# PSUM split, load order, single-tile groups, planned transfer times, PE transposes and zero matmuls in a fused attention and two-matrix kernel

## The chip, the cores and the metric

The kernel runs on one core of one Trainium2 chip. The metric is the device time in microseconds (us). Most quoted times are medians of several runs. Ratios to the kernel before are computed as the mean time of one kernel's fast runs over the mean time of the other's fast runs of the same rounds, so they are not quite the ratio of the medians. The profile shows the span from the first to the last instruction, which is about 1.8 us shorter than the device time.

PE is TensorE, ACT is ScalarE, DVE is VectorE, POOL is GpSimd, SP is SyncE. A "tile" in the text is a block of 128 tokens; there are 24 of them (4 batches of 768 tokens), numbered 0 to 23.

## The reference, cut to what matters

```python
# q, k, v: (4, 8, 768, 64)   w_in: (512, 2048)   w_out: (2048, 512)
scores = q @ k.T / 8 + bias                 # keep only the last 96 keys and the first 8
a = softmax(scores)
x = (a @ v) as (3072 tokens, 512)
h = x @ w_in                                # the "first matrix"
out = (h - tanh(h)) @ w_out                 # the "second matrix"
```

Because only the last 96 keys count, a tile's queries meet the keys of their own tile and of the tile before. So each tile has one or two blocks of scores for 8 heads.

## The kernel before

The kernel describes all its work as operations with an engine, a modelled duration, what they wait for and which buffers they take and give. A planner in the kernel (plain Python, run when it is built) simulates this and so fixes the order of instructions on each engine. Engines work strictly in that order. If the plan thinks that a transfer is done sooner than it is, PE stands before an instruction that can't run yet, though other work behind it could.

```python
groups = [[0, 1], [2, 3], [4, 5]] + [[u, u + 1, u + 2] for u in range(6, NU, 3)]
ps_big = ... bufs=3    # [P, 2, 512] fp32: two banks each
ps_sm  = ... bufs=1    # one bank: transposes, late AV
ps_op  = ... bufs=1    # one bank: second-matrix output, early AV
PE_T = 6               # tiles 0-5: q/k and x are transposed by PE, the rest by DMA
# ... cut ...
def m1(g, f0):         # first matrix of one group: a chunk fills two banks
    n, per, m = shape1(g)
    t = hs[g, f0] = ps_big.tile([P, 2, 512], FP32, name="big")
    # ... per f: CD = 4 matmuls over the contraction
# ... cut ...
AHEAD = 5.5
T_DT, T_DX = 1.0, 0.5                 # the plan's time of a q/k and of an x transpose by DMA
T_LD, T_W, T_ST = 1.15, 3.15, 0.7
before = [("t", 0), ("t", 1), ("t", 2), ("in", 0), ("t", 3), ("in", 1), ("in", 2), ("in", 3),
          ("out", 0), ("out", 1), ("t", 4), ("out", 2), ("out", 3), ("t", 5)]
```

The list `before` is the order of loads: `t` is a tile's q, k and v (3 x 256 KB), `in` and `out` are quarters of the two weight matrices. The first matrix of a group can start when x of all its tiles has been transposed. The Trainium skill, "PSUM — Partial Sum Buffer", section "Specifications (TRN2)", gives 8 banks of 2 KiB per partition. The kernel uses all of them: 3 x 2 + 1 + 1.

The softmax here doesn't subtract the row's maximum and nothing guards it: scores larger than these inputs give would overflow.

Of the kernel before, what the change touches and what calls it, by code (L numbers as in the profile page):

```python
# [16 lines left out]
def kernel(  # L17
# [14 lines left out]
    P = 128  # L32
# [15 lines left out]
    PE_T = 6  # L48
    TMAX = 3


    groups = [[0, 1], [2, 3], [4, 5]] + [[u, u + 1, u + 2] for u in range(6, NU, 3)]
# [13 lines left out]
    ps_big = ctx.enter_context(tc.tile_pool(name="ps_big", bufs=3, space=bass.MemoryType.PSUM))  # L66
    ps_sm = ctx.enter_context(tc.tile_pool(name="ps_sm", bufs=1, space=bass.MemoryType.PSUM))
    ps_op = ctx.enter_context(tc.tile_pool(name="ps_op", bufs=1, space=bass.MemoryType.PSUM))
# [4 lines left out]
    tmp01 = cpool.tile([P, P], FP32, name="tmp01")  # L73
# [9 lines left out]
    def build_masks():  # L83
        r0, r1, r2 = rmat[:, 0, :], rmat[:, 1, :], rmat[:, 2, :]
        nc.gpsimd.iota(
            r1, pattern=[[1, P]], base=0, channel_multiplier=-1,
            allow_small_or_imprecise_dtypes=True,
        )
        nc.gpsimd.tensor_copy(out=tmp01, in_=r1)
        nc.gpsimd.iota(  # L90
            r2, pattern=[[1, P]], base=P, channel_multiplier=-1,
            allow_small_or_imprecise_dtypes=True,
        )
        for dst, fill in ((r1, BIG), (tmp01, float(L))):
            nc.gpsimd.affine_select(
                dst, dst, pattern=[[1, P]], base=0, channel_multiplier=-1,
                compare_op=ALU.is_ge, fill=fill,
            )
            nc.gpsimd.affine_select(
                dst, dst, pattern=[[-1, P]], base=L - 1, channel_multiplier=1,  # L100
                compare_op=ALU.is_ge, fill=fill,
            )
        nc.gpsimd.affine_select(
            r2, r2, pattern=[[-1, P]], base=L - 1 - P, channel_multiplier=1,
            compare_op=ALU.is_ge, fill=BIG,
        )
        nc.gpsimd.memset(rmat[0:G, 2, :], float(L))
        nc.gpsimd.tensor_copy(out=r0, in_=r1)
        nc.gpsimd.tensor_copy(out=rmat[0:G, 0, :], in_=tmp01[0:G, :])
        for h in range(H):  # L110
            slope = 2.0 ** (-8.0 * (h + 1) / H)
            nc.scalar.activation(mk[:, slot(h), :, :], rmat, AF.Exp, bias=0.0, scale=-slope)
# [57 lines left out]
    def a_T(u):  # L170
        tr[u] = ps_sm.tile([P, 2, NP, P], BF16, name="sm")
        for j in (1, 0):
            for p in range(NP):
                nc.tensor.transpose(tr[u][:, j, p, :], kq[u][:, j, p * P : (p + 1) * P], ident)  # L174
# [7 lines left out]
    def a_Te(u):  # L182
        qk[u] = kpool.tile([P, 2, NP, P], BF16, name="qk")
        nc.vector.tensor_copy(out=qk[u], in_=tr.pop(u))
# [24 lines left out]
    def a_AV(u, part):  # L209
        h0 = part * (H // 2)  # L210
        pool, nm = (ps_op, "op") if u < AV_OP else (ps_sm, "sm")
        t = pool.tile([P, H // 2, Dh + 1], FP32, name=nm)
        for h in range(H // 2):
            last = u % NQ == 0
            nc.tensor.matmul(  # L215
                t[:, h, :], pr[u, 0][:, slot(h0 + h), :], vb[u % NV][:, h0 + h, :],
                start=True, stop=last,
            )
            if not last:
                nc.tensor.matmul(  # L220
                    t[:, h, :], pr[u, 1][:, slot(h0 + h), :], vb[(u - 1) % NV][:, h0 + h, :],
                    start=False, stop=True,
                )
        av[u, part] = t

    def a_R(u, part):
        h0 = part * (H // 2)
        if part == 0:
            xs[u] = xpool.tile([P, H, Dh], BF16, name="x")
        t = av.pop((u, part))  # L230
        rden = xpool.tile([P, H // 2, 1], FP32, name="rden")
        nc.vector.reciprocal(rden, t[:, :, Dh : Dh + 1])  # L232
        nc.vector.tensor_tensor(  # L233
            out=xs[u][:, h0 : h0 + H // 2, :], in0=t[:, :, 0:Dh],
            in1=rden.to_broadcast([P, H // 2, Dh]), op=ALU.mult,
        )

    def a_V(u):
        nc.gpsimd.tensor_copy(
            out=vb[u % NV][0:G, :, 0:Dh], in_=vb[(u - u % NQ) % NV][0:G, :, 0:Dh]  # L240
        )

    def a_X(u):
        x = xs[u].rearrange("q h d -> q (h d)")
        tr[u, "x"] = ps_sm.tile([P, CD, P], BF16, name="sm")
# [3 lines left out]
    def x_dst(u):  # L249
        g = group_of[u]  # L250
        if g not in xT:
            xT[g] = tpool.tile([P, CD, TMAX * P], BF16, name="xT")
        o = (u - groups[g][0]) * P
        return xT[g][:, :, o : o + P]
# [8 lines left out]
    gs, hs, ths, os_, ots = {}, {}, {}, {}, {}  # L263

    def shape1(g):
        n = len(groups[g]) * P
        per = 512 // n
        return n, per, min(2 * per, FJ)

    def m1(g, f0):  # L270
        n, per, m = shape1(g)
        t = hs[g, f0] = ps_big.tile([P, 2, 512], FP32, name="big")
        for f in range(f0, f0 + m):
            j, fo = f // FJ, (f % FJ) * P
            a, o = (f - f0) // per, ((f - f0) % per) * n
            for c in range(CD):
                nc.tensor.matmul(  # L277
                    t[:, a, o : o + n], w_in_bf[j][:, c, fo : fo + P], xT[g][:, c, 0:n],
                    start=(c == 0), stop=(c == CD - 1),
                )  # L280

    def h_view(t, g):
        n, per, m = shape1(g)
        per = min(per, m)
        return t[:, 0 : m // per, 0 : per * n].rearrange("q a (b n) -> q a b n", n=n)

    def m1_th(g, f0):
        ths[g, f0] = hpool.tile([P, 2, 512], FP32, name="th")
        nc.scalar.activation(h_view(ths[g, f0], g), h_view(hs[g, f0], g), AF.Tanh, bias=0.0, scale=1.0)  # L289

    def m1_g(g, f0):
        n, per, m = shape1(g)
        if g not in gs:
            gs[g] = gpool.tile([P, CF, TMAX * P], BF16, name="g")
        dst = gs[g][:, f0 : f0 + m, 0:n].rearrange("q (a b) n -> q a b n", b=min(per, m))
        nc.vector.tensor_tensor(  # L296
            out=dst, in0=h_view(hs.pop((g, f0)), g), in1=h_view(ths.pop((g, f0)), g), op=ALU.subtract,
        )

    def m2(g, t, qq):  # L300
        u = groups[g][t]
        if qq == 0:
            pool, nm = (ps_sm, "sm") if tail_sm(u) else (ps_op, "op")
            os_[u] = pool.tile([P, DM], FP32, name=nm)
        for f in range(qq * 4, qq * 4 + 4):
            nc.tensor.matmul(  # L306
                os_[u], gs[g][:, f, t * P : (t + 1) * P], w_out_bf[f // FJ][:, f % FJ, :],
                start=(f == 0), stop=(f == CF - 1),
            )

    def tail_sm(u):
        return u == NU - 2
# [5 lines left out]
    def store(u):  # L318
# [3 lines left out]
    AV_OP = 4  # L322
    AHEAD = 5.5
    T_DT, T_DX = 1.0, 0.5
    T_LD, T_W, T_ST = 1.15, 3.15, 0.7
    before = [("t", 0), ("t", 1), ("t", 2), ("in", 0), ("t", 3), ("in", 1), ("in", 2), ("in", 3),
              ("out", 0), ("out", 1), ("t", 4), ("out", 2), ("out", 3), ("t", 5)]
# [4 lines left out]
    for u in range(6, NU):  # L332
        gate_of["ld", "kf", u] = ("ld", "kf", u - 1)
    for n, it in enumerate(before):
        if n >= 2 and (it[0] == "t") != (before[n - 1][0] == "t"):
            gate_of[("ld", "kf", it[1]) if it[0] == "t" else it] = landed(before[n - 2])
    for it in before:
        if it[0] != "t":
            kind, j = it
            op(it, POOL, 0.8, (lambda j=j: load_w_in(j)) if kind == "in" else (lambda j=j: load_w_out(j)),  # L340
               after=[gate_of.get(it)], dma=T_W, pri=-1)
    w_order = [it for it in before if it[0] != "t"]
    for a, b in zip(w_order, w_order[1:]):
        ops[b]["after"].append(("issue", a))
# [3 lines left out]
    for g, us in enumerate(groups):  # L348
        n, per, m = shape1(g)
# [4 lines left out]
    tiles = [it[1] for it in before if it[0] == "t"]  # L354
    tiles += [u for u in range(NU) if u not in tiles]
    prev = None
    for u in tiles:
        i = u % NQ
# [5 lines left out]
    for u in range(NU):  # L364
        i = u % NQ
        e0 = DVE if u == 0 else POOL
        op(("ck", u), e0, 0.62, lambda u=u, e=e0: cast(u, 1, kf, nc.vector if e is DVE else nc.gpsimd),
           after=[("ld", "kf", u)], take=["kq"], give=["kf"])
        op(("cq", u), e0, 0.62, lambda u=u, e=e0: cast(u, 0, qf, nc.vector if e is DVE else nc.gpsimd),
           after=[("ld", "qf", u), ("ck", u)], give=["qf"])  # L370
        op(("cv", u), POOL, 0.62, lambda u=u: cast_v(u),
           after=[("ld", "vf", u), ("AV", u - NV + 1, 1) if u >= NV else None,
# [3 lines left out]
        if u < PE_T:  # L376
            op(("T", u), PE, 0.46, lambda u=u: a_T(u), after=tdep, take=["sm"], give=["kq"])
            op(("Te", u), DVE, 0.69, lambda u=u: a_Te(u), after=[("T", u)], give=["sm"])
        else:
            op(("T", u), SP, 0.3, lambda u=u: a_DT(u), after=tdep, give=["kq"], dma=T_DT)  # L380
        te = ("Te", u) if u < PE_T else ("T", u)
# [6 lines left out]
        if 1 <= i < NQ - 1:  # L388
            op(("K", u), DVE, 0.2, lambda u=u: a_K(u), after=[("S", u, 0)])
            op(("V", u), POOL, 0.61, lambda u=u: a_V(u), after=[("AV", u, 1)])  # L390
        for part in range(2):
            bank = "op" if u < AV_OP else "sm"
            op(("AV", u, part), PE, 0.25, lambda u=u, part=part: a_AV(u, part),
               after=[("M", u, 0), ("M", u, 1) if i else None, ("cv", u),
                      ("V", u - 1) if i >= 2 else None, ("AV", u, 0) if part else None],
               take=[bank], give=(["p0", "p1"] if i else ["p0"]) if part else [])
            op(("R", u, part), DVE, 0.63, lambda u=u, part=part: a_R(u, part), after=[("AV", u, part)],
# [150 lines left out]
```

## Time and profile before

| | before |
|---|---|
| device time, median of 3 (range) | 239.92 us (238.84 to 241.54) |
| span of the profiled run | 238.6 us |
| PE busy | 205.2 us (86%) |
| last matmul ends | 234.7 us |

Below are lines from the page's first two parts: the busy time of each engine, then PE, granted TensorE clock and DMA in tenths over 40 slices of the span, about 6 us each.

```profile
PE 205.2 (86%) x1712; PEld 122.6 (51%) x1736; DVE 127.4 (53%) x238; ACT 111.5 (47%) x137; POOL 64.9 (27%) x111
...
PE   1476876999999669979896997999999999999993
...
PEclk9999799999999999999999999999999999999999
DMA  7998998999999999899999999543342111111112
```

The windows view sums up stages. Its columns are the window, its length, then busy time (and number of instructions) of PE, weight loads, DVE, ACT, POOL, the granted clock, the DMA share and GB/s.

```profile
0.00:20.00 20.00, 9.16 (x98) 6.40 (x99) 9.75 (x30) 9.61 (x14) 11.52 (x28) 1.00 1.05 184
20.00:50.00 30.00, 24.65 (x237) 18.79 (x238) 16.49 (x28) 11.52 (x12) 9.55 (x15) 0.94 1.10 189
50.00:80.00 30.00, 27.18 (x276) 17.56 (x280) 18.86 (x38) 15.15 (x18) 13.73 (x22) 1.00 1.24 225
80.00:120.00 40.00, 33.94 (x323) 19.66 (x325) 26.41 (x52) 21.44 (x26) 14.89 (x24) 1.00 1.03 209
120.00:160.00 40.00, 36.16 (x308) 20.54 (x311) 23.80 (x46) 21.59 (x27) 13.39 (x21) 1.00 1.05 194
160.00:200.00 40.00, 39.63 (x305) 22.36 (x308) 22.48 (x39) 20.01 (x25) 1.83 (x3) 1.00 0.26 67
```

PE is the bound from 160 us on. Before that it waits: 10.8 us of the first 20, and 9.9 us between 80 and 160 us (80 less 33.94 and 36.16). DMA is busy until 150 us.

Busy does not mean fast. These are lines of the timeline (start, length, engine, line, operation, tiles, shape, count, and in brackets the idle time before and what ended it):

```profile
11.54 1.04 PE L192 MATMUL big<-qk 64*128 64x128 bf16 x16 [0.57 <-DVE qk L184]
...
19.72 3.24 PE L277 MATMUL big<-xT,w_in_bf_98 128*128 128x256 bf16 x16 [0.63 <-DVE xT L257]
...
43.02 1.91 PE L277 MATMUL big<-xT,w_in_bf_100 128*128 128x256 bf16 x16
...
77.37 0.62 PE L192 MATMUL big<-qk 64*128 64x128 bf16 x16
```

The same 16 matmuls take 3.24 us at 19.7 us and 1.91 us at 43 us; scores take 1.04 us early and 0.62 us later. The PEclk row above can't show this: the trace has no clock record before 22.5 us. (The prediction quotes 1.75 and 0.57 us for the later ones, from the chain of waits, which cuts a piece where the next begins.)

The waits view of PE (who waited for whom: total us, times, longest) names the DMA transpose of q and k before the scores first:

```profile
PE big L192 <- DMA qk<-kq: 7.4, 7, 1.8
```

### The profile page before, as it was taken

Reading aid. Unit: us, or ns where it says so; the run is one execution under the profiler, and the core shown is the slowest. Engines: PE = TensorE matmul, PEld = TensorE weight load, DVE = VectorE, ACT = ScalarE, POOL = GpSimd, SP = SyncE. Lnnn points to the kernel's source line nnn. Section 1 sums busy time; section 2 is a strip of 40 time slices with the busy share of each in tenths; the row PEclk is TensorE's granted clock in tenths of the full one; section 3 lists DMA queues with packets and bytes.
Section 4 is the critical chain, followed back from the end, with each engine's and each line's share of the span. In section 5 each row is a group of like instructions: output and inputs, shape, how many; then the busy total and the mean of one; then the engine's idle time right before and its main releaser. Section 6 shows DMA issues by size and latency. Waiting matters only on the chain.

```text
span 238.6 us, 4359 instructions
## 1 busy us (share of the span) xinstructions
PE 205.2 (86%) x1712; PEld 122.6 (51%) x1736; DVE 127.4 (53%) x238; ACT 111.5 (47%) x137; POOL 64.9 (27%) x111
## 2 busy tenths in 40 slices
PE   1476876999999669979896997999999999999993
PEld 0364565655676436536453554555555555555441
DVE  2464474863387757748673664665667443334300
ACT  4443061624276555648255635555665433243310
POOL 5638206054334453334442412331011000000000
PEclk9999799999999999999999999999999999999999
DMA  7998998999999999899999999543342111111112
GB/s 155 218 219 130 204 210 132 218 224 240 247 180 248 167 216 249 182 197 217 215 223 207 234 221 209 139 100 84 66 113 66 46 23 45 45 47 44 44 44 88
DMA packets 111380, 36.72 MB, mean 154 GB/s; under 512 B 104192, under 2 KB 108288, under 8 KB 111360
## 3 DMA queue, kind: packets, MB, share of 16 engines
q1 hardware_dynamic: 107136, 32.25, 67.9%
q0 software_dynamic: 4224, 4.19, 11.1%
q8 instruction: 13, 0.21, 0.4%
q14 instruction: 7, 0.06, 0.1%
HBM read 27.26 MB, written 6.29 MB: 141 GB/s over the span
## 4 chain that ended last, share of the span: by engine, by line
PE 66%; DMA 17%; DVE 6%; ACT 3%; SPq 3%; issue 2%; POOL 2%; ACTq 0%; POOLq 0%
PE big L277 29%; PE op L306 27%; DMA qk<-kq 6%; DMA qf<-in_q_dram 4%; PE big L192 4%; DMA vf<-in_v_dram 4%; SPq L148 2%; DVE g L296 2%; DMA kf<-in_k_dram 2%; PE sm L306 1%; DMA xT<-x 1%; ACT pd L200 1%; PE sm L174 1%; ACT ot L316 1%; PE sm L215 1%
## 5 line engine op out<-in xcount | busy, mean ns | idle before, releaser
L296 DVE TENSOR_TENSOR g<-big,th 128x768 bf16<-128x768 f32 (+1 forms) x60 | 60.5, 1010 | 50.4 <-ACT th L289 50.4
L289 ACT ACTIVATE th<-big 128x768 f32<-128x768 f32 (+1 forms) x60 | 51.3, 855 | 75.9 <-PE big L277 75.7
L306 PEld LDWEIGHTS <-g 128*128 128x128 bf16 x384 | 35.3, 98 | 38.4 <-issue 2.0
L200 ACT ACTIVATE pd<-big 128x1024 bf16<-128x1024 f32 x24 | 24.6, 1023 | 23.5 <-PE big L192 23.5
L162 POOL CAST kq<-kf 128x512 bf16<-128x512 f32 x23 | 15.1, 655 | 48.9 <-DMA kf<-in_k_dram 28.7
L277 PE MATMUL big<-xT,w_in_bf_98 128*128 128x384 bf16 (+1 forms) x144 | 24.5, 321 | 1.5 <-DMA xT<-x 0.9
L277 PE MATMUL big<-xT,w_in_bf_99 128*128 128x384 bf16 (+1 forms) x144 | 24.9, 324 | 0.0
L306 PE MATMUL op<-w_out_bf_102,g 128*128 128x512 bf16 x78 | 22.7, 379 | 2.5 <-ACT ot L316 1.5
L277 PE MATMUL big<-xT,w_in_bf_100 128*128 128x384 bf16 (+1 forms) x144 | 23.0, 308 | 1.5 <-ACT pd L200 1.5
L306 PE MATMUL op<-w_out_bf_105,g 128*128 128x512 bf16 x88 | 22.9, 379 | 1.3 <-DVE rden L232 1.1
L192 PE MATMUL big<-qk 64*128 64x128 bf16 x352 | 15.6, 228 | 9.1 <-DMA qk<-kq 7.4
L306 PE MATMUL op<-w_out_bf_103,g 128*128 128x512 bf16 x89 | 23.2, 380 | 0.2 <-issue 0.2
L277 PE MATMUL big<-xT,w_in_bf_101 128*128 128x384 bf16 (+1 forms) x144 | 23.3, 308 | 0.1
L306 PE MATMUL op<-w_out_bf_104,g 128*128 128x512 bf16 x89 | 23.1, 379 | 0.2
L204 DVE TENSOR_TENSOR pd<-pd,mk 128x1024 bf16<-128x1024 bf16 x24 | 17.0, 708 | 11.0 <-ACT pd L200 11.0
L316 ACT COPY ot<-op 128x512 f32<-128x512 f32 x23 | 13.5, 588 | 18.4 <-PE op L306 16.8
L200 ACT ACTIVATE po<-big 128x1024 bf16<-128x1024 f32 x20 | 20.4, 1022 | 0.0
L277 PEld LDWEIGHTS <-w_in_bf_98 128*128 128x128 bf16 x144 | 14.3, 102 | 9.7 <-DMA xT<-x 1.0
L215 PEld LDWEIGHTS <-pd 128*128 128x128 bf16 x192 | 14.8, 101 | 7.4 <-DVE x L233 2.6
L192 PEld LDWEIGHTS <-qk 64*128 64x128 bf16 x352 | 10.6, 99 | 15.5 <-DMA qk<-kq 10.2
L277 PEld LDWEIGHTS <-w_in_bf_101 128*128 128x128 bf16 x144 | 14.0, 98 | 8.1
L277 PEld LDWEIGHTS <-w_in_bf_100 128*128 128x128 bf16 x144 | 13.8, 98 | 8.5 <-issue 1.5
(104 smaller groups left out, 191.5 us busy)
## 6 DMA issues: line engine op xcount, KB each, us to landing
kf<-in_k_dram SPq DMA_DIRECT2D x24, 256.0 KB, 3.8
qf<-in_q_dram SPq DMA_DIRECT2D x24, 256.0 KB, 4.4
vf<-in_v_dram SPq DMA_DIRECT2D x24, 256.0 KB, 4.8
out_dram<-ot SPq DMA_DIRECT2D x24, 256.0 KB, 2.5
w_in_bf_98<-in_moe_w_in_dram POOLq DMA_DIRECT2D x1, 512.0 KB, 5.7
w_in_bf_99<-in_moe_w_in_dram POOLq DMA_DIRECT2D x1, 512.0 KB, 5.4
w_in_bf_100<-in_moe_w_in_dram POOLq DMA_DIRECT2D x1, 512.0 KB, 7.9
w_in_bf_101<-in_moe_w_in_dram POOLq DMA_DIRECT2D x1, 512.0 KB, 9.7
```

Of the source, the lines that this page charges most:

```text
L148: started(("ld", nm, u), nc.sync.dma_start(out=dst[u], in_=src[b, :, i * P : (i + 1) * P, :].rearrange("h p d -> p h d")))
L162: eng.tensor_copy(out=kq[u][:, j, :], in_=src.pop(u).rearrange("p h d -> p (h d)"))
L174: nc.tensor.transpose(tr[u][:, j, p, :], kq[u][:, j, p * P : (p + 1) * P], ident)
L192: nc.tensor.matmul(s[:, slot(2 * p + hh), :], qk[u - o][r, 1, p, :], qk[u][r, 0, p, :], start=True, stop=True,)
L200: nc.scalar.activation(pr[u, o], s, AF.Exp, bias=0.0, scale=scale)
L204: nc.vector.tensor_tensor(out=pr[u, o], in0=pr[u, o], in1=mk[:, :, m, :], op=ALU.mult)
L215: nc.tensor.matmul(t[:, h, :], pr[u, 0][:, slot(h0 + h), :], vb[u % NV][:, h0 + h, :], start=True, stop=last,)
L277: nc.tensor.matmul(t[:, a, o : o + n], w_in_bf[j][:, c, fo : fo + P], xT[g][:, c, 0:n], start=(c == 0), stop=(c == CD - 1),)
L289: nc.scalar.activation(h_view(ths[g, f0], g), h_view(hs[g, f0], g), AF.Tanh, bias=0.0, scale=1.0)
L296: nc.vector.tensor_tensor(out=dst, in0=h_view(hs.pop((g, f0)), g), in1=h_view(ths.pop((g, f0)), g), op=ALU.subtract,)
L306: nc.tensor.matmul(os_[u], gs[g][:, f, t * P : (t + 1) * P], w_out_bf[f // FJ][:, f % FJ, :], start=(f == 0), stop=(f == CF - 1),)
L316: nc.scalar.copy(out=ots[u], in_=os_.pop(u))
```

## The change

The intent is to keep PE fed while loads arrive, and to plan with transfer times that are nearer to what the chip shows. It has these parts:

- Loads: tiles 0 to 3 first, then all eight weight quarters, then tiles 4 to 6.
- Groups: tiles 0 to 5 go through the first matrix one by one, and their work may be interleaved by the weight quarter that has landed. The later groups stay trios (three tiles each).
- PSUM: two 2-bank buffers for scores and AV and four 1-bank buffers for everything else, 2 x 2 + 4. A first-matrix chunk fills one bank, so there are 120 tanh instructions instead of 60.
- Planned times: a q/k transpose by DMA 1.75 instead of 1.0 us, an x transpose 0.9 instead of 0.5, head start 5.0 instead of 5.5 tiles.
- PE transposes q/k of tiles 0 to 7 and x of tiles 0 to 8, instead of 0 to 5 for both.
- Zero matmuls fill PE's planned gaps in the first 19 us.
- Smaller ones: the masks are built by DVE, AV of a tile is one operation, ACT takes over half of the copy after PE's q/k transposes, small copies move from POOL to DVE, and the rules that hold back loads differ.

```diff
-    PE_T = 6
+    PE_T, PE_X = 8, 9
-    groups = [[0, 1], [2, 3], [4, 5]] + [[u, u + 1, u + 2] for u in range(6, NU, 3)]
+    EARLY, EARLY2 = 6, 4
+    groups = [[u] for u in range(EARLY)] + [[u, u + 1, u + 2] for u in range(EARLY, NU, HT)]
-    ps_big = ... bufs=3
-    ps_sm = ... bufs=1
-    ps_op = ... bufs=1
+    ps_big = ... bufs=2
+    ps_one = ... bufs=4
 # ... cut: masks, AV and its division in one operation, copies on DVE ...
+    def warm():
+        if not warm_bank:
+            warm_bank.append(ps_one.tile([P, 512], FP32, name="one"))
+        nc.tensor.matmul(warm_bank[0], zero[:, 0:P], zero, start=True, stop=True)
     def m1(g, f0):
-        t = hs[g, f0] = ps_big.tile([P, 2, 512], FP32, name="big")
+        t = hs[g, f0] = ps_one.tile([P, 512], FP32, name="one")
 # ... cut ...
-    AHEAD = 5.5
-    T_DT, T_DX = 1.0, 0.5
-    T_LD, T_W, T_ST = 1.15, 3.15, 0.7
-    before = [("t", 0), ("t", 1), ("t", 2), ("in", 0), ("t", 3), ("in", 1), ("in", 2), ("in", 3),
-              ("out", 0), ("out", 1), ("t", 4), ("out", 2), ("out", 3), ("t", 5)]
+    AHEAD = 5.0
+    WARM = (1.4, 19.0)
+    T_LD, T_W, T_ST, T_DT, T_DX = 1.15, 3.15, 0.7, 1.75, 0.9
+    before = [("t", 0), ("t", 1), ("t", 2), ("t", 3), ("in", 0), ("in", 1), ("in", 2), ("in", 3),
+              ("out", 0), ("out", 1), ("out", 2), ("out", 3), ("t", 4), ("t", 5), ("t", 6)]
 # ... cut: the planner takes matrix work of tiles 0-5 from one queue per tile ...
```

## The prediction

> **What bounds it now.** Three stages. (a) 0 to 40 us: loading. The windows view gives PE 23.9 us busy of 40, much of it at half speed: 16 score matmuls take 1.04 us at 11.5 us and 0.57 us at 77.4 us; a first-matrix chunk takes 3.24 us at 19.7 us and 1.75 us at 43.2 us. DMA is saturated (about 200 GB/s): tile 3 lands at 19.4 us, then weight pieces about 2.7 us apart, tile 4 at 38.2, two pieces, tile 5 at 49.3. With two-tile groups PE has little to do meanwhile. (b) 40 to 160 us: PE about 88% busy; the waits view names the transposing DMA before the scores (PE <- qk, 7 waits, 7.4 us) and short waits for VectorE/ScalarE; the plan thought a transpose takes 1.0 us, they land 3.6 us after issue. (c) 160 to 235 us: PE over 98% busy. After the last matmul 3.9 us of copy and store.
>
> PE work at full clock, from chunk times: first matrix 83, second 24 x 3.46 = 83, scores 12.5, AV 12, transposes 4: about 195 us of a 238.6 us span. 43 us are lost: about 25 by 40 us, 14 from 40 to 235, 4 at the end.
>
> **What the change moves.** Tiles 0 to 3 land first, 1.2 us per load, the last at about 17 us (estimate). Weight pieces follow about 2.9 us apart, at about 20 to 40 us; tile 4 at about 44. Single-tile groups let PE use each piece at once on up to four tiles: 4 x 3.5 us of first matrix plus 4 x 3.46 of second fill PE from 20 to 50 us, with no gap over 1 us. By 50 us PE has done about 34 us of work instead of 25: gain 9 us.
>
> Zero matmuls: the Trainium skill, "TensorE: Matmul & The Clock Gate", Part 1, has PE at half clock until about 3.4 us of sustained activity; this trace agrees (1.04 against 0.57 us). They should hold the clock at 1.0 from about 6 us. In the DMA-paced first 20 us that is hidden, but the first chunks then run at full speed (counted above).
>
> Mid stage: the plan's longer DMA times put scores later; I give back 5 of the 8 us of DMA waits. But only two 2-bank buffers remain for scores and AV: new short waits (+2 us). PE gains 2 q/k and 3 x transposes: +1.6 us.
>
> 60 tanh chunks become about 120. From the measured sizes (1024: 1025 ns, 768: 812 ns) fixed cost is about 0.17 us: ScalarE from 111 to about 124, VectorE to about 134. Neither reaches 60% of the span; not critical.
>
> **Sum.** 239.9 - 9 (early) - 5 (DMA waits) + 2 (banks) + 1.6 (PE) - 2 (starvation gaps 50 to 80 us) = about 227 us. Range 220 to 234.
>
> **What would show it.** Right: weight pieces landing from 20 to 40 us; clock row all 9s from 10 us; PE over 90% busy in 20 to 50 us; PE waits on qk under 4 us; (c) and tail unchanged. Wrong: PE gaps of 2 us or more between 20 and 55 us, or PE waiting for ScalarE copies or first-matrix buffers.
>
> **What would make it wrong.** Tile 4 comes later (44 against 38 us): if its attention chain (some 6 us) doesn't fit under the second-matrix work, up to 5 us are lost at 50 us. One-bank chunks could make ScalarE/VectorE latency visible in (c): 0.2 us on each of 96 chunks would eat the gain. Zero matmuls could delay the first tiles. Chances: faster by over 2% 0.88, within 2% 0.09, slower 0.03.

## More of the kernel before

The chain of waits, in order of time, shows the start of the first group of three tiles (6 to 8), called the first trio:

```profile
86.26 3.30 DMA xT<-x
89.56 0.05 issue
89.61 2.77 PE big L277 x16
```

## The result, and the profile after

The kernel after takes 226.19 us (median of 3, 225.73 to 226.70). The ratio of its fast runs to those of before is 0.942 (95% interval 0.933 to 0.951). A later run on another chip, under experiment e9, gave 225.8 us (6 runs) and 0.937 (0.932 to 0.942).

| | before | after |
|---|---|---|
| device time, median | 239.92 us | 226.19 us |
| span of the profiled run | 238.6 us | 224.4 us |
| sixth output tile copied | 86.0 us | 77.0 us |
| first trio starts | 89.6 us | 77.7 us |
| last matmul ends | 234.7 us | 220.8 us |

The same lines of the page after:

```profile
PE 211.9 (94%) x1975; PEld 126.0 (56%) x1998; DVE 136.4 (61%) x279; ACT 124.2 (55%) x205; POOL 53.8 (24%) x85
...
PE   6898899999899999899999999999999999999993
...
PEclk9999999999999999999999999999999999999999
DMA  7999999999999999999999999997514121011112
```

The same stages in the windows view. PE's 16.66 us of the first 20 contain the zero matmuls.

```profile
0.00:20.00 20.00, 16.66 (x145) 8.76 (x147) 11.25 (x36) 11.92 (x18) 9.17 (x19) 1.00 1.11 186
20.00:50.00 30.00, 28.63 (x385) 22.01 (x387) 16.13 (x30) 14.30 (x23) 7.51 (x11) 1.00 1.07 183
50.00:80.00 30.00, 28.30 (x376) 19.73 (x376) 22.82 (x44) 18.96 (x28) 13.42 (x19) 1.00 1.18 225
80.00:120.00 40.00, 38.37 (x348) 21.49 (x349) 30.06 (x62) 25.54 (x44) 12.31 (x19) 1.00 1.19 219
120.00:160.00 40.00, 39.58 (x352) 22.12 (x357) 28.47 (x58) 25.37 (x43) 11.35 (x17) 1.00 1.04 189
160.00:200.00 40.00, 39.74 (x277) 21.81 (x281) 22.17 (x44) 20.74 (x39) 0.00 (x0) 1.00 0.21 56
```

PE is 95% busy from 20 to 50 us (28.63 of 30), and between 80 and 160 us it now waits 2.0 us instead of 9.9. Waits for q/k transposes are gone. The longest totals in PE's waits view are:

```profile
PE big L217 <- DVE po L202: 1.2, 3, 0.7
...
PE one L240 <- DVE x L226: 1.0, 3, 0.4
PE one L273 <- DVE xT L249: 0.9, 2, 0.7
PE one L273 <- DMA w_in_bf_97<-in_moe_w_in_dram: 0.8, 1, 0.8
```

The first trio's last x transpose is now done by PE and copied by DVE. In the chain of waits:

```profile
76.98 0.24 PE one L240 x4
77.24 0.43 DVE xT L249
77.67 0.04 issue
77.72 2.44 PE one L273 x14
```

The first trio is a good milestone. In both kernels, all matrix work of tiles 0 to 5 is finished when it starts (the sixth copy comes just before) and all matrix work of tiles 6 to 23 is still to do. The 14.2 us between the spans divide there: 11.9 us come before the trio starts (89.6 less 77.7), 2.0 us from there to the last matmul (145.1 less 143.1), and 0.3 us in the tail. After it, the kernel before has less attention left: 22 blocks of scores and 160 AV matmuls are behind it, against 18 and 128 (counted in the traces). Four blocks at about 0.29 us and 32 AV matmuls at about 0.034 us make 2.2 us. So the waits after the trio fell by about 4 us, not by 2, and of the 11.9 us before it about 2.2 are attention that was put off.

### The profile page after: what moved, and what is told of

It reads as the page before. It is cut to its first block, busy times and chain, and to the rows that moved or that the text cites. A ratio compares the mean times of both kernels' runs of the same rounds, so it can differ in the third digit from the quotient of the medians.

```text
span 224.4 us, 5020 instructions
## 1 busy us (share of the span) xinstructions
PE 211.9 (94%) x1975; PEld 126.0 (56%) x1998; DVE 136.4 (61%) x279; ACT 124.2 (55%) x205; POOL 53.8 (24%) x85
## 4 chain that ended last, share of the span: by engine, by line
PE 78%; DMA 7%; SPq 6%; DVE 3%; ACT 3%; issue 1%
PE one L273 35%; PE one L300 34%; SPq L143 5%; PE big L190 4%; DMA w_in_bf_97<-in_moe_w_in_dram 3%; DMA vf<-in_v_dram 3%; PE big L213 2%; PE big L217 2%; DMA xT<-x 2%; ACT pd L198 2%; DVE po L202 1%; DVE pd L202 1%; PE one L240 1%; PE one L169 1%; DVE xT L249 1%
## 5 line engine op out<-in xcount | busy, mean ns | idle before, releaser
L284 ACT ACTIVATE th<-one 128x384 f32<-128x384 f32 (+1 forms) x120 | 60.7, 516 | 51.7 <-PE one L273 47.7
L290 DVE TENSOR_TENSOR g<-one,th 128x384 bf16<-128x384 f32 (+1 forms) x120 | 67.6, 579 | 32.7 <-ACT th L284 30.7
L300 PEld LDWEIGHTS <-g 128*128 128x128 bf16 x384 | 36.0, 98 | 36.0
L198 ACT ACTIVATE pd<-big 128x1024 bf16<-128x1024 f32 x24 | 24.6, 1024 | 16.6 <-PE big L190 14.9
L307 ACT COPY ot<-one 128x512 f32<-128x512 f32 x24 | 14.1, 587 | 23.9 <-PE one L300 23.8
L202 DVE TENSOR_TENSOR pd<-pd,mk 128x1024 bf16<-128x1024 bf16 x24 | 18.4, 768 | 11.9 <-ACT pd L198 11.5
L273 PE MATMUL one<-xT,w_in_bf_96 128*128 128x128 bf16 (+1 forms) x192 | 24.6, 273 | 1.1 <-DVE xT L249 0.9
L273 PE MATMUL one<-xT,w_in_bf_97 128*128 128x128 bf16 (+1 forms) x192 | 24.7, 273 | 0.8 <-DMA w_in_bf_97<-in_moe_w_in_dram 0.8
L273 PE MATMUL one<-xT,w_in_bf_99 128*128 128x128 bf16 (+1 forms) x192 | 25.2, 273 | 0.0
L273 PE MATMUL one<-xT,w_in_bf_98 128*128 128x128 bf16 (+1 forms) x192 | 25.1, 273 | 0.0
L300 PE MATMUL one<-w_out_bf_100,g 128*128 128x512 bf16 x88 | 24.1, 379 | 0.5 <-issue 0.2
L300 PE MATMUL one<-w_out_bf_103,g 128*128 128x512 bf16 x94 | 24.1, 379 | 0.2
L300 PE MATMUL one<-w_out_bf_101,g 128*128 128x512 bf16 x92 | 23.8, 379 | 0.2
L300 PE MATMUL one<-w_out_bf_102,g 128*128 128x512 bf16 x89 | 23.1, 379 | 0.4 <-issue 0.2
L273 PEld LDWEIGHTS <-w_in_bf_96 128*128 128x128 bf16 x192 | 14.6, 98 | 9.1 <-issue 1.3
L273 PEld LDWEIGHTS <-w_in_bf_99 128*128 128x128 bf16 x192 | 14.8, 98 | 7.4
L273 PEld LDWEIGHTS <-w_in_bf_97 128*128 128x128 bf16 x192 | 14.4, 98 | 7.9 <-DMA w_in_bf_97<-in_moe_w_in_dram 1.0
L273 PEld LDWEIGHTS <-w_in_bf_98 128*128 128x128 bf16 x192 | 14.6, 98 | 7.2
L157 POOL CAST kq<-qf 128x512 bf16<-128x512 f32 x23 | 15.6, 678 | 10.0 <-DMA qf<-in_q_dram 9.9
L202 DVE TENSOR_TENSOR po<-po,mk 128x1024 bf16<-128x1024 bf16 x20 | 15.9, 797 | 3.0 <-ACT po L198 3.0
```

The lines of the kernel that those rows point to most:

```text
L157: eng.tensor_copy(out=kq[u][:, j, :], in_=src.pop(u).rearrange("p h d -> p (h d)"))
L198: nc.scalar.activation(pr[u, o], s, AF.Exp, bias=0.0, scale=scale)
L202: nc.vector.tensor_tensor(out=pr[u, o], in0=pr[u, o], in1=mk[:, :, m, :], op=ALU.mult)
L273: nc.tensor.matmul(t[:, (f - f0) * n : (f - f0 + 1) * n], w_in_bf[j][:, c, fo : fo + P], xT[b][:, c, o : o + n], start=(c == 0), stop=(c = ...
L284: nc.scalar.activation(h_view(ths[g, f0], g), h_view(hs[g, f0], g), AF.Tanh, bias=0.0, scale=1.0)
L290: nc.vector.tensor_tensor(out=gs[b][:, f0 : f0 + m, o : o + n], in0=h_view(hs.pop((g, f0)), g), in1=h_view(ths.pop((g, f0)), g), op=ALU.su ...
```

## The experiments

Twelve runs were made, one of them of the unchanged kernel after. All outputs were correct. The "after" to compare with has a ratio of 0.937 (six runs) or 0.942 (three runs). The profile of e7 and one more of its four runs are slow, and so are one run each of e3 and e12. One note on the milestone: in e6 and e10 a part of tile 5's second matrix is still to do when the first trio starts (the sixth copy comes at 81.4 and 95.0 us), so their last column flatters them.

| run | what | ratio to before (95%) | first trio starts |
|---|---|---|---|
| e9 | after, unchanged | 0.937 (0.932 to 0.942) | 77.1 us |
| e1 | after, one zero matmul only | 0.945 (0.940 to 0.949) | 80.1 us |
| e2 | after, trios from the start | 0.971 (0.965 to 0.976) | |
| e3 | after, loads as before | 0.949 (0.940 to 0.958) | 78.5 us |
| e4 | after, planned times as before | 0.979 (0.971 to 0.986) | 78.3 us |
| e6 | after, first matrix in 2-bank chunks | 0.946 (0.936 to 0.955) | 77.2 us |
| e7 | after, PE transposes six tiles | 0.967 (0.956 to 0.978) | 88.4 us |
| e5 | before, planned times as after | 0.992 (0.984 to 1.000) | 89.7 us |
| e10 | e5, PE transposes nine tiles | 0.972 (0.967 to 0.978) | 85.0 us |
| e11 | e7 with zero matmuls in its waits | 0.973 (0.967 to 0.979) | 87.7 us |
| e8 | after, first weight quarter earlier | 0.941 (0.933 to 0.949) | 79.2 us |
| e12 | e8, looser gates on loads | 0.946 (0.940 to 0.951) | 79.7 us |

### e9: the standard

No edit. It was run beside e10 to e12 to have after and before on one chip.

> The kernel after, unchanged, as the standard for the other runs of this chip. Ratio to before as at first, 0.942 (0.935 to 0.950); first-matrix work of the first trio (tiles 6 to 8) starts at 77 to 79 us.

It came out as expected: 225.8 us, ratio 0.937.

### e1: what the zero matmuls are worth

```diff
-                ops["warm", n] = dict(eng=PE, us=us, fn=warm)
-                order.append((last, ("warm", n)))
+                if n == 0:
+                    ops["warm", n] = dict(eng=PE, us=us, fn=warm)
+                    order.append((last, ("warm", n)))
```

> The kernel after with all but the first zero matmul left out; order, buffers and everything else unchanged. Theory (clock): PE stays at half speed until it has had some us of real first-matrix work from about 21 us on; the 32 first-matrix matmuls at 21.4 us take about 3.5 us instead of 1.8 us, part of it in the wait for the second weight piece (lands 24.7 us). Expected 228 us, about 2 us over after. Rival 1 (hidden): everything before 24 us waits for loads anyway, so no difference (under 0.5 us). Rival 2 (the clock is the early gain): 4 us or more over after, about half of the 7.6 us by which after is ahead at 50 us.

The median is 227.7 us (227.6 to 228.6), about 2 us over after, and the ratio differs by 0.003 to 0.008. The clock records say full clock from 25.8 us on, against 4.3 us in after. The order of instructions is the same, so the traces can be laid side by side: the first trio starts at 80.1 instead of 77.7 us, the last matmul ends at 222.3 instead of 220.8 us. The size fits the clock theory best and speaks against 4 us or more. By the ratios alone (0.6 to 1.8 us) rival 1 isn't excluded; the traces speak against it. These are the first first-matrix matmuls, in e1 and then in after:

```profile
23.65 2.95 PE L273 MATMUL one<-xT,w_in_bf 128*128 128x128 bf16 x32
```

```profile
21.44 1.96 PE L273 MATMUL one<-xT,w_in_bf_96 128*128 128x128 bf16 x32
```

They start 2.2 us later in e1, although its first weight piece landed a little earlier (19.6 against 20.3 us). From 10 to 23.7 us the chain of waits of e1 runs through the attention of the first tiles, on PE at half clock (8 score matmuls take 0.61 instead of 0.40 us), on ACT and on DVE; that of after runs through loads. So with a low clock the work before the first matrix is not hidden behind the loads. The half-speed chunk itself costs 1.0 us more (2.95 against 1.96 us), but after then waits 0.8 us for the second weight piece. Here e1 and after ran on different chips, so the 2 us are good to perhaps 1 us.

### e2: single tiles or trios

```diff
-    EARLY, EARLY2 = 6, 4
+    EARLY, EARLY2 = 0, 4
```

> The kernel after with groups of three tiles from the start; loads, banks, zero matmuls as in after. Theory (single tiles feed PE while weights land): the second trio needs tile 5, which lands near 50 us, so PE has only one trio's 21 us of matrix work between 23 and 55 us and stands idle for some 7 us before 57 us: 233 us, 6 to 8 us over after. Rival (load order and clock are enough): within 2 us of after.

The median is 234.2 us, 8 us over after. This is the windows view of the stage after the weights have landed:

```profile
20.00:50.00 30.00, 26.87 (x201) 14.91 (x199) 14.84 (x30) 12.87 (x23) 8.15 (x12) 0.94 1.23 192
50.00:64.00 14.00, 9.62 (x99) 7.22 (x99) 8.78 (x18) 6.15 (x9) 7.05 (x10) 0.52 1.07 240
```

From 50 to 64 us PE has little to do until tile 5 is ready, and it does that little at about half the clock. The fourth output tile is copied at 85.2 us, against 53.6 us in after. The theory holds: the loss is of the expected size and lies in the expected place.

### e3: the order of loads

```diff
-    before = [("t", 0), ("t", 1), ("t", 2), ("t", 3), ("in", 0), ("in", 1), ("in", 2), ("in", 3),
-              ("out", 0), ("out", 1), ("out", 2), ("out", 3), ("t", 4), ("t", 5), ("t", 6)]
+    before = [("t", 0), ("t", 1), ("t", 2), ("in", 0), ("t", 3), ("in", 1), ("in", 2), ("in", 3),
+              ("out", 0), ("out", 1), ("t", 4), ("out", 2), ("out", 3), ("t", 5)]
```

> The kernel after with the loads in the order of before (third weight piece on after tile 3, tile 4 between the weights). Theory: with single-tile groups the PE can use any order; tile 3 comes 2 us later, weights 2 and 3 about as before; 1 to 3 us over after, 228.5 us. Rival (the load order is the early gain): 5 us or more over after.

The fast runs are 227.8, 227.9 and 230.8 us, so 2 to 5 us over after. The load order probably helps, by roughly what the theory said, though the intervals of the two ratios overlap (0.940 to 0.958 against 0.932 to 0.942); the rival's 5 us or more isn't seen in two of the three fast runs.

### e4 and e5: the planned times, undone in after and done alone in before

Both edits change the head start together with the two times; what each is worth alone was not tried.

e4, on after:

```diff
-    AHEAD = 5.0
-    T_LD, T_W, T_ST, T_DT, T_DX = 1.15, 3.15, 0.7, 1.75, 0.9
+    AHEAD = 5.5
+    T_LD, T_W, T_ST, T_DT, T_DX = 1.15, 3.15, 0.7, 1.0, 0.5
```

> The kernel after with the plan's old transfer times and head start (1.0, 0.5, 5.5 instead of 1.75, 0.9, 5.0); nothing else. Theory (the plan's times removed the PE waits for transposing DMAs): PE waits for qk come back, some 5 us: 231 us. Rival (banks, or the better early stage, removed them): within 1.5 us of after.

The median is 236.0 us, about 10 us over after, twice what was expected. The first trio starts at 78.3 us, as early as in after; the whole loss lies behind it (152.8 us from there to the last matmul, instead of 143.1). The cause is what the theory names. PE's waits view:

```profile
PE big L190 <- DMA qk<-kq: 9.4, 9, 2.0
```

e5, on before:

```diff
-    AHEAD = 5.5
-    T_DT, T_DX = 1.0, 0.5
+    AHEAD = 5.0
+    T_DT, T_DX = 1.75, 0.9
```

> The kernel before with the new plan's transfer times and head start alone (1.75, 0.9, 5.0). Theory (the plan's times cause the PE waits for transposing DMAs, 8 us between 85 and 152 us): 5 us faster than before, 235 us, PE waits on qk under 3 us. Rival (they come from elsewhere): within 1.5 us of before.

The waits for q/k transposes vanish from PE's view altogether, but the ratio is only 0.992, about 2 us (0 to 4 by its interval). That is a miss for the theory as it stood. The trace shows where the rest went: the sixth output tile is copied at 82.9 us instead of 86.0, but the first trio starts at 89.7 us as before. In between, PE has run out of matrix work and waits for VectorE in the attention of the next tiles; and x of tile 8, which the trio needs, lands only at 88.9 us. From the timeline of e5:

```profile
86.79 0.20 PE L215 MATMUL sm<-vb,pd 128*128 128x65 bf16 x1 [1.62 <-DVE pd L204]
87.94 0.24 PE L220 MATMUL sm<-vb,po 128*128 128x65 bf16 x1 [0.94 <-DVE po L204]
89.24 0.24 PE L215 MATMUL sm<-vb,pd 128*128 128x65 bf16 x1 [0.74 <-DVE x L233]
```

So the same two lines are worth about 2 us in one kernel and 10 us in the other. What holds in both is that they remove the q/k waits; what that is worth depends on what stands next.

### e7: how many tiles PE transposes

```diff
-    PE_T, PE_X = 8, 9
+    PE_T, PE_X = 6, 6
```

> The kernel after with PE transposing only the first six tiles, as before (6, 6 instead of 8, 9); five transposes go back to DMA, which saves PE 1.6 us. Theory: within 1.5 us of after, since PE work falls by 1.6 us and tiles 6 to 8 wait some us longer for a busy DMA. Rival (the PE transposes are what removed the gaps between 50 and 90 us): 3 us or more over after.

The fast runs are 232.3 and 233.2 us, about 7 us over after. The theory, that these transposes cost PE 1.6 us and bring little, fell; the rival holds. The sixth output tile is copied at 75.7 us, a little earlier than in after. But then the first trio doesn't start. The timeline of e7:

```profile
87.42 1.04 PE L190 MATMUL big<-qk 64*128 64x128 bf16 x16 [4.05 <-DMA qk<-kq]
88.39 0.50 PE L273 MATMUL one<-xT,w_in_bf 128*128 128x384 bf16 x1
```

It starts at 88.4 us, 12.7 us after the copy, where in after it is 0.7 us. The wait shown is for q and k of tile 10, whose scores stand before the trio in PE's order; x of tile 8 lands at 87.9 us, so the trio was hardly ready sooner. This profile is of a slow run, but e11 below, which has the same transposes and a fast profile, starts the trio at 87.7 us. With the transposes of tiles 6 to 8 left to DMA, the first trio starts between 87.7 and 89.7 us in before, e5, e7 and e11, whatever PE finishes before it. With PE transposing them it starts at 77.7 us. A DMA transpose takes a median of 3.6 to 4.3 us from issue to landing for q and k, and 2.6 to 3.7 us for x (DMA views of before, after and e7); PE and VectorE need 0.7 us for x in the chain shown above. Which of the two, q/k of tiles 6 and 7 or x of tiles 6 to 8, matters more was not tried. But the traces show that the transpose of tile 8's x is only the last part: VectorE has finished that x at 84.6 us in e7 and at 76.0 us in after. So some 8.5 of the 10.7 us are lost before it, in the attention of tiles 6 to 8. Even q and k of tile 8, which go by DMA in both kernels, land at 73.4 instead of 69.4 us.

### e10: the same on the other side

```diff
 # e5, and:
-    PE_T = 6
+    PE_T = 9
```

> The kernel before with the new plan's times (as in e5) and with PE transposing q, k and x of tiles 0 to 8 instead of 0 to 5. Theory (formed from e5 and e7: between 70 and 90 us PE runs out of matrix work, because the first trio needs tile 8, whose DMA transposes land late; it starts at 89.7 us in e5 and at 77.7 us in after): the trio starts at about 80 us and the ratio to before falls from 0.992 to about 0.965 (233 us on a chip where before takes 241). Rival (tiles 6 to 8 are late for other reasons, such as their loads or the single transpose bank of before): ratio 0.985 or more, trio at 86 us or later.

The ratio is 0.972, between the expectation (0.965) and the rival (0.985 or more) and nearer to the first. The trio starts at 85.0 us, 4.7 us earlier than in e5 and not the 10 us that the theory hoped for, and half of tile 5's second matrix is still behind it. With the early stage of before, the matrix work of tiles 0 to 5 is itself late (in e10 the fifth copy comes at 82.2 us). So the transposes help before as well, until the next thing binds.

### e11: does the half clock in the middle cost anything by itself?

e7's clock is half from 80.5 to 90.7 us, and this looked like a cost of its own. The edit adds 28 zero matmuls where PE waits there, written where later matmuls overwrite:

```diff
+    NZ = {("S", 9, 0): 2, ("S", 10, 0): 14, ("AV", 7, 1): 5, ("AV", 8, 0): 4, ("AV", 8, 1): 3}
+    def zeros(dst, *key):
+        for _ in range(NZ.get(key, 0)):
+            nc.tensor.matmul(dst, zero[:, 0:P], zero, start=True, stop=True)
 # called before the scores and within AV of these tiles
```

> e7 (PE transposes only six tiles) with 28 zero matmuls put where PE waited in e7 between 76 and 87 us (before scores of tiles 9 and 10, before and within AV of tiles 7 and 8), written where later matmuls overwrite. In e7 the granted clock is half from 80.5 to 90.7 us. Theory (half the clock is a cost of its own on top of the waits): no dip, the trio's first chunks at 88.4 us run at full speed, some 2 us faster than e7: ratio 0.959. Rival (the dip falls where PE waits anyway): within 0.7 us of e7, ratio 0.967.

The mean granted clock rose: 0.991 to 0.993 in all four runs, against 0.971 to 0.978 in e7's. The dip shrank from 10.2 to 3.4 us. But the time didn't fall: 233.4 to 235.6 us against 232.3 and 233.2 us in e7's fast runs (on another chip), and the trio starts at 87.7 us. So the 2 us that the theory promised did not come. But the test isn't clean, as the timeline of e11 shows:

```profile
82.37 4.87 PE L188 MATMUL big<-zero 128*128 128x512 bf16 x14
```

These are the zeros before the scores of tile 10. They run at half clock themselves for 3.4 us and end at 87.2 us, while q and k of tile 10 had landed at 85.9 and x of tile 8 at 86.3 us. So the zeros held PE up by about 1 us. In e7 PE is busy for only 4.55 of the 10.2 us of the dip, so half the clock can have lengthened its matmuls by about 2.3 us (an estimate: half of 4.55); 16 matmuls of the trio take 3.91 us there and 2.77 us in e11. What the dip costs by itself stays open, from nothing to about 2 us.

### e6: the banks

```diff
-    ps_big bufs=2, ps_one bufs=4;  plan: "big": 2, "one": 4, "mo": 3
+    ps_big bufs=3, ps_one bufs=2;  plan: "big": 3, "one": 2, "mo": 1
-        return ..., n, 512 // n
+        return ..., n, min(2 * (512 // n), FJ)
-        t = hs[g, f0] = ps_one.tile([P, 512], FP32, name="one")
+        t = hs[g, f0] = ps_big.tile([P, 2, 512], FP32, name="big")
 # and the views of h, tanh(h) and g to match
```

> The kernel after with the PSUM of before for the first matrix: three 2-bank and two 1-bank buffers, first-matrix chunks of two banks in the 2-bank buffers; loads, single tiles, zero matmuls and the plan's times as in after. Theory of the prediction (the new banks cost 2 us of short waits): 2 us faster to 1 us slower than after, 224 to 227 us. Rival (the banks are a main source of the gain, since the second matrix's outputs, transposes and chunks no longer queue for single buffers): 4 us or more over after.

The runs are 226.2 to 229.0 us, ratio 0.946 with an interval that reaches from 0.936 to 0.955. This fits neither expectation clearly: the banks are not a main source of the gain, and the predicted cost of 2 us doesn't show either. Their worth, anything between 0 and about 3 us of gain, stays open. The price of the smaller chunks does show in the groups view. Before, then after (columns: line, engine, operation, tiles, shapes, count, busy us, mean ns, idle before and who ended it):

```profile
L296 DVE TENSOR_TENSOR g<-big,th 128x768 bf16<-128x768 f32 (+1 forms) x60 | 60.5, 1010 | 50.4 <-ACT th L289 50.4
L289 ACT ACTIVATE th<-big 128x768 f32<-128x768 f32 (+1 forms) x60 | 51.3, 855 | 75.9 <-PE big L277 75.7
```

```profile
L284 ACT ACTIVATE th<-one 128x384 f32<-128x384 f32 (+1 forms) x120 | 60.7, 516 | 51.7 <-PE one L273 47.7
L290 DVE TENSOR_TENSOR g<-one,th 128x384 bf16<-128x384 f32 (+1 forms) x120 | 67.6, 579 | 32.7 <-ACT th L284 30.7
```

ACT pays 9.4 us more and DVE 7.1 us more for the same elements. Neither is the bound, so this is free here.

### e8 and e12: tries at a better kernel

e8:

```diff
-    before = [("t", 0), ("t", 1), ("t", 2), ("t", 3), ("in", 0), ("in", 1), ...
+    before = [("t", 0), ("t", 1), ("in", 0), ("t", 2), ("t", 3), ("in", 1), ...
```

> A try at a better kernel: after, with the first weight piece loaded after tile 1 instead of after tile 3. Theory (in the first 20 us PE lacks weights, not tiles): first-matrix work of tiles 0 and 1 starts at about 14 to 18 us instead of 21.4 us; 1 to 2 us faster than after, 224.5 us. Rival (the early stage is bound by tiles' chains or PE from 25 us on, so earlier work only moves idle time): within 0.7 us of after, or slower, since tiles 2 and 3 come 2.8 us later.

Its ratio is 0.941 and its median 226.0 us: no better than after. The first matrix does start earlier, at 12.9 instead of 21.4 us, but PE then waits for weight pieces between 26 and 45 us (1.9 us in four waits), and the first trio starts at 79.2 us. (The profile is of its slowest run, 228.4 us.) The rival holds: earlier work only moved idle time.

e12:

```diff
 # e8, and:
-            gate_of[...] = landed(before[n - 2])
+            gate_of[...] = landed(before[max(n - 3, 0)])
```

> A second try at a better kernel: e8 (first weight piece after tile 1) with each gated load held back by the load three places before it instead of two, so that the DMA queues stay fuller. Theory (in e8 PE then waited for weight pieces and did less work from 20 to 50 us): pieces land earlier, the last near 40 us instead of 42.5 us or later; 1 to 2 us faster than after on the same chip, ratio 0.937. Rival (DMA is saturated either way, so more in flight only delays tiles 2 and 3): same as after or slower, ratio 0.942 or more.

Its ratio is 0.946, against 0.937 for after on the same chip: slower. Against e8, from which it differs by the gate alone, the last weight piece landed 0.8 us sooner (43.6 instead of 44.4 us, on another chip), but tile 3 landed 3.8 us later (25.3 instead of 21.5 us). With the load order of after, in e9, the last piece landed at 41.8 us. The rival holds again. After is the best of the kernels that ran.

## Why the prediction was right, and where its parts were wrong

The total was right: 227 us predicted, 226.2 us measured. Its parts fare as follows.

- **Early stage, "by 50 us PE has done about 34 us of work instead of 25: gain 9 us".** Right in kind, a little large. By 50 us both kernels have started first-matrix matmuls for four tiles' worth of columns (128 of 256 columns before, 256 of 128 after). For the second matrix the traces count 13 before and 48 after. 35 more at 0.216 us (3.46 us for 16) are 7.6 us; the trace of e9, the same kernel as after with fewer records missing, counts 52, so 8 us is nearer. PE was over 90% busy from 20 to 50 us, as said. e2 shows that this rests on the single-tile groups.
- **Loads.** Tile 3 landed at 17.9 us (17 predicted), the weight pieces from 20.3 to 42.5 us (20 to 40), tile 4 at 47.0 us (44). The feared gap at 50 us was small: two PE waits of 0.37 and 0.73 us around 55 us.
- **Zero matmuls.** The rule of the Trainium skill, "TensorE: Matmul & The Clock Gate", Part 1, is near what the traces show: full clock from 4.3 us in after, 3.1 us after the first zero matmul at 1.2 us, but only from 6.8 us in e9, the same kernel, 5.6 us after it. (The trace that the prediction quotes shows two speeds, not how long the change takes.) By e1 the zero matmuls are worth about 2 us. One step was wrong: the prediction called the first 20 us hidden behind the loads, and in e1 the first-matrix work begins 2.2 us late because attention ran at half clock.
- **"I give back 5 of the 8 us of DMA waits."** The mechanism was right: the waits went, all of them. The size was off: the change of times and head start alone was worth about 2 us in e5, and taking it back cost 10 us in e4. There is no one number for it.
- **"PE gains 2 q/k and 3 x transposes: +1.6 us."** This is the step that failed. The transposes do cost PE time, but the first trio starts some 10 us earlier with them, and undoing them cost 7 us (e7). The prediction booked only a vague 2 us for "starvation gaps". Had the change left them out, the early gain would have been spent waiting for the first trio.
- **"Only two 2-bank buffers remain: new short waits (+2 us)."** Not seen; e6 leaves open whether the banks are worth nothing or a little.
- **ScalarE about 124, VectorE about 134 us, not critical; late stage and tail unchanged.** 124.2, 136.4, and a tail of 3.6 instead of 3.9 us. Right.

That the sum came out is partly luck: a gain that was booked as a cost and a gain that was too small stood against items that were too large. The parts don't add up in any case. Undoing them one at a time costs, in parts of the time before and from the ratios above less 0.937: 0.008 (e1), 0.034 (e2), 0.012 (e3), 0.042 (e4), 0.030 (e7), 0.009 (e6), each uncertain by 0.005 to 0.01. Together that is 0.135, about twice the gain of 0.063. My reading, argued and not tested by itself: they all feed one queue of matrix work in front of PE, and if any one is missing, PE waits at that place and part of the others' gain is lost there.

## What to carry to other kernels

Find a milestone that splits the work in the same way in both kernels (here the start of the first trio) and compare when each reaches it; this told in one look which stage an edit had helped. When a kernel feeds one engine through a fixed order, ask of each early gain what the next piece of work waits for: in e7 tiles 0 to 5 were done ten microseconds sooner than before, and the first trio started only 1.2 us sooner. An operation that costs the busiest engine time can still shorten the whole, if it takes a slower path out of the chain that feeds that engine.

## What the Trainium skill lacked or had wrong

- "TensorE: Matmul & The Clock Gate", Part 1, doesn't say whether zero operands count as activity for the clock gate. Here they do: full clock from 4.3 us with the zero matmuls (6.8 us in e9, the same kernel, whose trace counts 42 of them in the first 20 us), from 25.8 us with one (e1).
- The same part warns that the clock records are not always to be trusted. Here the profile gives a clock of 1.00 for 0 to 20 us before, while 16 score matmuls took 1.04 instead of 0.62 us; there was simply no record before 22.5 us. Matmul lengths decide.
- The same page, section "Terms", puts the penalty of a throttled stage at its length times the lost share, which is 5.1 us for e7's dip of 10.2 us. But PE was busy for only 4.55 us of that dip, so its matmuls there can have been longer by about 2.3 us at most (an estimate: half of 4.55). In this case the formula counts waiting too.
- The same page, Part 4, says that full clock doesn't engage for PE transposes. Eight of them took 1.01 us at 14.6 us in before and 0.61 us at 50.3 us in after, so these do run faster where other work has raised the clock. Whether transposes alone raise it was not tried, and the trace lists them as MATMUL and doesn't tell their mode.
- "DMA: Bandwidth & Descriptors", section "DMA Transpose (X-bar)", gives no time for one transpose of these sizes beside other traffic. Here 128 x 1024 bf16 (q and k) took a median of 3.6 to 4.3 us from issue to landing, and 128 x 512 (x) 2.6 to 3.7 us. A plan with 1.0 and 0.5 us and the longer head start cost 10 us (e4).
